# Output products as swapped 64-row halves in the common loop, an exchanged query order in pair 14, and the last norm in pieces

## The chip, the cores and the metric

The kernel runs on one core of a Trainium2 chip. Its engines are TensorE (PE in the profile, its weight loads PEld), VectorE (DVE), ScalarE (ACT), GpSimd (POOL) and SyncE (SP), which only issues DMAs here. Each takes its instructions in program order, and they wait for one another by semaphores. The metric is the device time of one execution in microseconds.

## The reference, cut to what matters

```python
x = A_x                              # 1 x 2048 x 576, 32 heads of 18
xn = layernorm(x)
q, k, v = split(xn @ wqkv)
p = softmax(q @ k.T * 18 ** -0.5)    # per head, 2048 x 2048
s = concat_heads(p @ v) @ wo
h = gelu(xn @ w_gate) * (xn @ w_up)  # 4608 wide
g = silu(h @ w_down)
return x + s * g
```

## The kernel before, in words

All products of 576-wide operands are made from 16-bit high and low parts, three matmuls in place of one. The 2048 rows are 16 row tiles of 128 (`st`), four row blocks of 512 (`sb`). The 32 heads are worked in 16 pairs (`p`), one head on partitions 0 to 63, the other on 64 to 127.

For a pair there are 64 steps (`i`): query half `qh` of 1024 rows, key tile `kt` of 128, and `half`, one of two blocks of 512 queries. In each step `qk2` (lines 1298 to 1312) makes the scores of both heads, two matmuls of 56 rows at 1302 that run at the same time, and ScalarE takes the exponential at 1308. In the common loop for the first 15 pairs (line 1580) a step also holds `qk1` (the next pair's scores again, for the row maxima, 1245 to 1253), some slots of the gate and up projection (`g_run`, `Pair`, line 472), and now and then a stage of a down projection (`DownPair`, line 762). `make_plan` (1536) lays out from a cost table how many slots and down stages each of the next steps gets, so that the gate stream ends `LEAD` steps after step 960, the end of the fifteenth pair. When a gate pair closes, the key tiles held in `pend` go through `burst` (1333): the products of P and V, four column groups of 32, in 32-bit, added on VectorE into `osum`.

A `Pair` or `DownPair` computes two results from 64-row halves. In its first stage the lower half of the array works on result a and the upper half on b, at the same time; in the second stage they change over. Between the stages stands `touch` (436), a copy of one element from PSUM on VectorE, on which the second stage waits.

At the end of a query half `norm` (1356) divides by the softmax sum (row 18 of each group). For pairs up to 13, and for the first half of the others, a chain of deferred small DMAs spreads the reciprocals (a1, a2, b, b1, b2), then c, d and e make high and low parts, and f stores them to the DRAM buffer OHL. For the second half of pairs 14 and 15 it is done in place (`direct`): a shuffle and a reciprocal of 128 x 512 on VectorE, then c, d, e at once. For pair 15 the parts stay in SBUF (`last_o`).

The last pair has a loop of its own (1658), behind `stage.open("c")`: every third step P times V by `pv` (1316), left-over down products by `down` (710, 128-row matmuls at 724), the gate's tanh and product (`queue_gate`, 800) one at a time, and, when all down products are done, the output products of `unit_out` (892) as a filler: for row tiles 8 to 15 those of pairs 0 to 14, for 0 to 5 also those of pair 15 from `last_o` (`mm_direct`, 870, line 877). An output product is 14 matmuls of 128 rows for each half of 288 columns (`mm_xw`, 486, lines 491 to 496), into one of three banks; at 923 VectorE multiplies by the gate, at 927 it adds x. Behind the loop come row tiles 6 and 7, and `final_out` (955) adds pair 15's share to row tiles 8 to 15.

Of the kernel before, what the change touches and what calls it, by code (L numbers as in the profile page):

```python
# [20 lines left out]
P = 128  # L21
# [14 lines left out]
T_XW = 0.123  # L36
TAIL_QC = 3
TAIL_K = 3
T_LAST = (NT * 28 + NT // 2 * 6 - (4 - TAIL_QC) * 2 * 34) * 0.123

# [58 lines left out]
def kernel(ctx: ExitStack, tc: tile.TileContext, x, wqkv, wo, w_gate, w_up, w_down, out):  # L99
# [610 lines left out]
    def down(tag):  # L710

        if not dnq:
            return False
        w, c, sb, si, hf = dnq.popleft()
        hs = hstate[c, sb]
        st = 4 * sb + si
        sl = slice(P * si, P * si + P)
        ms = slice(288 * hf, 288 * hf + 288)
        mt = MTile(tag, [P, 512], F32, 1)
        yy = Y[0][:, st, ms]  # L720
        k = 0
        for ft in range(2):
            for a, b in ((hs.hi, w.dhi), (hs.hi, w.dlo), (hs.lo, w.dhi)):
                nc.tensor.matmul(
                    mt.t[:, 0:288], a[:, ft, sl], b[:, ft, ms], start=(k == 0), stop=(k == 5)
                )
                k += 1
        if c == 0:
            nc.vector.tensor_scalar(yy, mt.t[:, 0:288], w.c, None, op0=ALU.mult)
        else:  # L730
            nc.vector.scalar_tensor_tensor(yy, mt.t[:, 0:288], w.c, yy, op0=ALU.mult, op1=ALU.add)
        mt.done()
        hs.left -= 1
        if hf == 1:
            dndone[c] += 1
            if c == NCH - 1 and si == 3:
                queue_gate(sb)
        return True

# [60 lines left out]
    def queue_gate(sb):  # L800

        for st in range(4 * sb, 4 * sb + 4):
            def e1(st=st):
                t = sgt[st] = stage.s.tile([P, D], F32, tag="sg", name=f"sg{st}", bufs=2)
                nc.scalar.activation(t, Y[0][:, st], AF.Tanh, scale=0.5)

            def r1(st=st):
                yy = Y[0][:, st]
                nc.vector.scalar_tensor_tensor(yy, sgt[st], 1.0, yy, op0=ALU.add, op1=ALU.mult)
                gdone[st] = 1  # L810

            gq.append(e1)
            gq.append(r1)

    sgt = {}
    gq = deque()
# [48 lines left out]
    ohl_here = []  # L865
    outk = [0]
    last_o = {}
    obt = {}

    def mm_direct(o, qh, qb, si, hf, start, stop, end=None):  # L870

        r = slice(64 * qb, 64 * qb + 64)
        sl = slice(P * si, P * si + P)
        ms = slice(288 * hf, 288 * hf + 288)
        oh, ol = last_o[qh]
        for k, (a, b) in enumerate(((oh, wod.hi), (oh, wod.lo), (ol, wod.hi))):
            nc.tensor.matmul(o, a[r, sl], b[r, ms], start=start and k == 0, stop=stop and k == 2)
            if k == 2 and end is not None:
                end()
            yield T_XW  # L880

# [3 lines left out]
    def load_ohl(qc):  # L885
        if qc in ohls:
            return
# [4 lines left out]
    def unit_out(qc, whole):  # L892

        qh = qc // 4
        until(lambda: obdone[qh] == NPAIR - 1 and W_O[0] is not None)
        if whole:
            until(lambda: qh in last_o)
        w = W_O[0]
        load_ohl(qc)
        k = OUT_ORDER.index(qc) + 1  # L900
        if k < len(OUT_ORDER):
            load_ohl(OUT_ORDER[k])
        ohl = ohls[qc]
        oh, ot, ol = ohl[:, 0:4], ohl[:, 4], ohl[:, 5:9]
        yield 0.0
        for si in range(2):
            st = 2 * qc + si
            sl = slice(P * si, P * si + P)
            xo = stage.s.tile([P, D], F32, tag="xo", name=f"xo{st}", bufs=2)
            nc.sync.dma_start(xo, x[P * st:P * st + P, :])  # L910
            if whole:
                ob = stage.s.tile([P, D], F32, tag="sg", name=f"ob{st}", bufs=2)
            else:
                ob = OB(st)
            for hf in range(2):
                ms = slice(288 * hf, 288 * hf + 288)
                mt = MTile(("ma", "mb", "mc")[outk[0] % 3], [P, 512], F32, 1)
                outk[0] += 1

                def fin(mt=mt, st=st, ms=ms, hf=hf, xo=xo, ob=ob):  # L920
                    while not gdone[st]:
                        gq.popleft()()
                    nc.vector.scalar_tensor_tensor(
                        ob[:, ms], mt.t[:, 0:288], EO, Y[0][:, st, ms], op0=ALU.mult, op1=ALU.mult
                    )
                    mt.done()
                    nc.vector.tensor_tensor(ob[:, ms], ob[:, ms], xo[:, ms], op=ALU.add)
                    if hf == 1 and whole:
                        nc.gpsimd.dma_start(out[P * st:P * st + P, :], ob)

                yield from mm_xw(
                    mt.t[:, 0:288], lambda t: oh[:, t, sl], lambda t: ol[:, t, sl], ot[:, sl], w, hf,
                    stop=not whole, end=None if whole else fin,
                )
                if whole:
                    yield from mm_direct(
                        mt.t[:, 0:288], qh, (qc % 4) // 2, st % 4, hf, False, True, fin
                    )
# [16 lines left out]
    def final_out(st):  # L955
        o = ps.tile([P, 2, 512], F32, tag=("s1", "s2")[st % 2], name=f"fo{st}")
        for hf in range(2):
            for _ in mm_direct(o[:, hf, 0:288], 1, (st - 8) // 4, st % 4, hf, True, True):
                pass
        t = ap.tile([P, D], F32, tag="P", name=f"ft{st}", bufs=6)  # L960
        nc.vector.scalar_tensor_tensor(
            t.rearrange("p (a b) -> p a b", a=2), o[:, :, 0:288], EO,
            Y[0][:, st].rearrange("p (a b) -> p a b", a=2), op0=ALU.mult, op1=ALU.mult,
        )
        eng = (nc.gpsimd, nc.vector)[st % 2]
        eng.tensor_tensor(t, t, OB(st), op=ALU.add)
        (nc.sync, nc.scalar)[st % 2].dma_start(out[P * st:P * st + P, :], t)
# [322 lines left out]
    def ptile(p, name):  # L1290
# [3 lines left out]
        if p < NPAIR - 1 and n < 64 * (NPAIR - 1) - 8 and n % 8 >= 6:  # L1294
# [19 lines left out]
    ob = [None]  # L1314

    def pv(p, qh, kt, pa, pb):
        if kt == 0:
            ob[0] = stage.p.tile([P, 512], F32, tag="pv", name=f"pv_{p}_{qh}")
        o = ob[0]
        for b, pt in enumerate((pa, pb)):  # L1320
            for h in range(2):
                qd = 64 * b + 32 * h
                c0 = 38 * kt + 19 * h
                nc.tensor.matmul(  # L1324
                    o[qd:qd + 32, :], VT[p][:, c0:c0 + 32], pt[:, h],
                    start=(kt == 0), stop=(kt == NT - 1), skip_group_check=True,
                )
        if kt == NT - 1:
            norm(p, qh, o)

    osum = {}

    def burst(todo, tag):
# [19 lines left out]
        if k1 == NT - 1:  # L1353
            norm(p, qh, None)
# [385 lines left out]
```

## Time and profile before

| | us |
|---|---|
| median of three runs (2620.77 to 2622.93) | 2620.93 |
| the profiled execution | 2621.11 |
| its span, first to last instruction | 2619.3 |
| first scores of the last pair | 2442.36 |
| last output product of the stream | 2601.86 |
| last addition (line 966) ends | 2615.83 |

The granted TensorE clock of the core is 0.992 over the span. In the profile's lists a row of the time-ordered view has start, duration, engine, line, operation and, in brackets, the idle time of the engine ahead of it with what ended it; matmul durations overlap, so what one costs is read from the distance to the next start.

### The profile page before, as it was taken

How to read it: one execution, taken by the hardware profiler on the slowest of the kernel's cores; microseconds unless marked ns; L12 is line 12 of the kernel's file. 1: busy time of each engine (PE TensorE's matmuls, PEld its weight loads, DVE VectorE, ACT ScalarE, POOL GpSimd, SP SyncE). 2: the span in 40 equal slices, each digit the busy share in tenths (PEclk: the TensorE clock that was granted, in tenths of full speed). 3: DMA queues.
4: the chain of work that ended last, by engine and by line, in shares of the span. 5: the costliest groups of instructions: out<-in, count | busy, mean ns of one | idle time of the engine just before them, and what ended most of it. 6: DMA issues, size and time to landing. Idle time of an engine off the chain costs nothing.

```text
span 2619.3 us, 59543 instructions
## 1 busy us (share of the span) xinstructions
PE 2526.9 (96%) x25220; PEld 1315.2 (50%) x25220; DVE 1930.7 (74%) x2714; ACT 1662.9 (63%) x2083; POOL 1487.4 (57%) x1418
## 2 busy tenths in 40 slices
PE   6889999999999999999999999999999999999898
PEld 5554545445545454454544554454454555555344
DVE  7587768777877778777887777777777777777444
ACT  5225666666677666767767676677666676766563
POOL 4246553576437553757667575756666575747301
PEclk9999999999999999999999999999999999999998
DMA  4430022202130022112021110102012011100123
GB/s 144 133 109 10 16 28 78 64 18 56 29 80 20 9 54 64 29 39 56 9 56 29 33 33 15 56 10 56 11 35 47 17 28 39 49 9 11 35 78 118
DMA packets 133640, 118.61 MB, mean 45 GB/s; under 512 B 60160, under 2 KB 112792, under 8 KB 133372
## 3 DMA queue, kind: packets, MB, share of 16 engines
q1 hardware_dynamic: 127740, 103.02, 15.2%
q0 software_dynamic: 3072, 8.90, 1.0%
q8 instruction: 197, 3.23, 0.5%
q10 hardware_dynamic: 2560, 2.89, 0.3%
q14 instruction: 71, 0.58, 0.1%
HBM read 84.89 MB, written 29.61 MB: 44 GB/s over the span
## 4 chain that ended last, share of the span: by engine, by line
PE 77%; DVE 10%; ACT 4%; DMA 3%; POOL 3%; issue 3%; SPq 0%; ACTq 0%; DVEq 0%; POOLq 0%
PE mb_t L472 15%; PE ma_t L472 14%; PE md_t L762 14%; PE s L1302 8%; PE md_t L1343 7%; PE s L1250 7%; PE ma_t L1343 5%; DVE PM L1253 3%; ACT P L1308 1%; DMA obr<-rd 1%; PE pv L1324 1%; DMA QT<-QD 1%; PE mc_t L491 1%; DVE m_c L252 1%; DVE osb L1351 1%
## 5 line engine op out<-in xcount | busy, mean ns | idle before, releaser
L1253 DVE TENSOR_REDUCE PM<-s 128x2 f32<-128x1024 f32 x1024 | 1250.8, 1224 | 340.4 <-PE s L1250 332.2
L1308 ACT ACTIVATE P<-s,etab 128x1024 f32<-128x1024 f32 x896 | 996.8, 1112 | 621.4 <-PE s L1302 606.1
L472 PE MATMUL ma_t<-XHT,whi_c 64*128 64x512 f16 x1440 | 542.4, 377 | 12.5 <-ACT gs L637 7.8
L472 PE MATMUL mb_t<-XHT,whi_c 64*128 64x512 f16 x1440 | 542.2, 377 | 5.2 <-ACT gv L648 2.7
L472 PE MATMUL ma_t<-XHT,wlo_c 64*128 64x512 f16 x1296 | 487.4, 376 | 0.0
L472 PE MATMUL ma_t<-XL,whi_c 64*128 64x512 f16 x1152 | 433.4, 376 | 0.0
L472 PE MATMUL mb_t<-XHT,wlo_c 64*128 64x512 f16 x1152 | 433.3, 376 | 0.0
L472 PE MATMUL mb_t<-XL,whi_c 64*128 64x512 f16 x1152 | 433.2, 376 | 0.0
L1250 PE MATMUL s<-KT,QT 54*128 54x512 f16 x2048 | 398.0, 378 | 18.5 <-DVE PM L1253 8.3
L1302 PE MATMUL s<-QT,KT 56*128 56x512 f16 x2048 | 401.0, 380 | 7.1 <-ACT P L1308 3.0
L472 PEld LDWEIGHTS <-whi_c 64*128 64x128 f16 x5184 | 276.9, 94 | 244.0 <-issue 31.8
L762 PE MATMUL md_t<-dhi_c,hhi 64*128 64x288 f16 x2216 | 327.5, 283 | 8.1 <-DVE osb L1351 5.3
L673 POOL TENSOR_SCALAR tw<-tw 128x512 f32<-128x512 f32 x144 | 90.8, 630 | 421.4 <-ACT tw L666 421.2
L762 PE MATMUL md_t<-dhi_c,hlo 64*128 64x288 f16 x2216 | 327.2, 283 | 0.0
L762 PE MATMUL md_t<-dlo_c,hhi 64*128 64x288 f16 x2216 | 326.7, 282 | 0.0
L762 PEld LDWEIGHTS <-hhi 64*128 64x128 f16 x4432 | 236.9, 94 | 137.0 <-issue 21.1
L695 POOL TENSOR_TENSOR hlo<-gv,hhi 128x512 f16<-128x512 f32 x144 | 168.6, 1171 | 225.2 <-ACT hhi L688 211.4
L1343 PE MATMUL md_t<-P,VT 128*32 128x512 f32 x2368 | 274.4, 596 | 0.4 <-DVE y L782 0.3
L1302 PEld LDWEIGHTS <-KT 56*128 56x128 f16 x2048 | 124.8, 94 | 263.0 <-issue 175.4
L660 POOL TENSOR_TENSOR tw<-gs 128x512 f32<-128x512 f32 x144 | 152.0, 1056 | 120.9 <-ACT gs L637 120.5
L782 DVE SCALAR_TENSOR_TENSOR y<-md_t,c_c,y 128x576 f32<-128x576 f32 x261 | 210.5, 806 | 1.2 <-PE md_t L762 1.2
L472 PEld LDWEIGHTS <-wlo_c 64*128 64x128 f16 x2592 | 139.6, 94 | 120.2 <-issue 1.0
(271 smaller groups left out, 4048.4 us busy)
## 6 DMA issues: line engine op xcount, KB each, us to landing
draw_c<-in_B_w_down SPq DMA_DIRECT2D x18, 576.0 KB
raw_c<-in_B_w_gate SPq DMA_DIRECT2D x18, 512.0 KB
raw_c<-in_B_w_up SPq DMA_DIRECT2D x18, 512.0 KB
obr<-rd SPq DMA_DIRECT2D x30, 256.0 KB
KT<-KD SPq DMA_DIRECT2D x32, 224.0 KB
QT<-QD SPq DMA_DIRECT2D x32, 216.0 KB
VS<-vst POOLq DMA_DIRECT2D x16, 304.0 KB, 3.8
VT<-VS SPq DMA_DIRECT2D x16, 304.0 KB
```

What stands on the lines that cost most here:

```text
L252: nc.vector.tensor_reduce(w.m5[:, t:t + 1], w.raw[:, t], op=ALU.max, axis=AX.XY, apply_absolute_value=True)
L472: nc.tensor.matmul(o, lw, xx, start=self.stage == 0 and self.k == 0, stop=self.stage == 1 and self.k == self.slots - 1, skip_group_check=True,
L660: gp.tensor_tensor(st["t"], st["g"], st["g"], op=ALU.mult)
L673: gp.tensor_scalar(st["t"], st["t"], 1.0, 1.0, op0=ALU.mult, op1=ALU.add)
L695: gp.tensor_tensor(hs.lo[:, ft], st["v"], hs.hi[:, ft], op=ALU.subtract)
L762: nc.tensor.matmul(self.t.t[:, hf, 0:288], a[r, ft, sl], b[r, ft, 288 * hf:288 * hf + 288], start=self.stage == 0 and k == 0, stop=self.st ...
L782: nc.vector.scalar_tensor_tensor(yy, y, w.c, yy, op0=ALU.mult, op1=ALU.add)
L1250: nc.tensor.matmul(s1[:, h], QT[p][r, P * qt:P * qt + P], KT[p][r, 512 * kb:512 * kb + 512], start=True, stop=True)
L1253: nc.vector.tensor_reduce(PM[p][:, :, qt, kb:kb + 1], s1, op=ALU.max, axis=AX.X)
L1302: nc.tensor.matmul(s2[:, h], KT[p][r, P * kt:P * kt + P], QT[p][r, 512 * qb:512 * qb + 512], start=True, stop=True)
L1308: nc.scalar.activation(pt, s2, AF.Exp, scale=ETAB[j0])
L1343: nc.tensor.matmul(t.t[qd:qd + 32, :], VT[p][:, c0:c0 + 32], pt[:, h], start=kt == k0, stop=kt == k1, skip_group_check=True,)
```

## The change

The loop of the last pair goes: the common loop runs over all 16 pairs. When the gate stream has ended, a step takes a branch of its own, with at most one down stage and some output slots.

- `LEAD` is 0 in place of 10, and the planner's choice of steps for a gate pair has slightly other bounds.
- In pair 14 the query halves are worked in exchanged order (`qh = 1 - qh`). Its norms both go through the deferred chain.
- The output products are `OutPair` objects: 64-row halves, two stages of 14 slots (17 with pair 15's terms, which stand on one half alone), a `touch` between them. Units take turns in PSUM: one wide tile `md`, or `ma` and `mb`. The product with the gate stays on VectorE, the addition of x goes to POOL (a whole row tile), the stores of row tiles 0 to 7 to SP's queue.
- A gate's tanh and product are issued in the same step, on odd steps.
- The norm of pair 15 is nine pieces (shuffle, four reciprocals of 128 columns, c, d, e, g), popped one in a step, two per stage behind the loop.
- `final_out` pairs row tiles 8 + k and 12 + k, whose terms stand on different halves, and six of its eight additions run on POOL.
- Buffers: sigmoid tiles and outputs in the QT buffers, x in the KT buffers, P tiles of the last pair also in PX.

```diff
+            self.q = []
+            for half in range(2):
+                hf = half ^ self.stage
+                r = slice(64 * half, 64 * half + 64)
+                terms = []
+                for t in range(4):
+                    for xx, ww in ((oh, w.hi), (oh, w.lo), (ol, w.hi)):
+                        terms.append((xx[r, t, sl], ww[r, t, hf, :]))
+                terms += [(ot[r, sl], w.hi[r, 4, hf, :]), (ot[r, sl], w.lo[r, 4, hf, :])]
+                if self.whole and half == st % 8 // 4:
+                    terms += direct_terms(st, hf)
+                self.q.append((self.o[hf], terms))
...
+            if self.stage == 0:
+                if self.wide:
+                    touch(self.t[0].t[0:1, :, 0:1])
+                else:
+                    for o in self.o[1:] if last else self.o[::-1]:
+                        touch(o[0:1, 0:1])
+            self.stage += 1
+            if self.stage == 2:
+                self.evac()
...
+        def evac(self):
+            st = self.st
+            while not gdone[st]:
+                for fn in gq.popleft():
+                    fn()
...
+            nc.gpsimd.tensor_tensor(ob, ob, self.xo, op=ALU.add)
+            if self.whole:
+                nc.sync.dma_start(out[P * st:P * st + P, :], ob)
```

The readiness of a unit, the pacing, and the branch of a step behind the gate stream (`more` is true up to pair 14):

```diff
+    def out_ready(st):
+
+        if st // 4 not in gated or obdone[st // 8] < NPAIR - 1 or W_O[0] is None:
+            return False
+        return st >= 8 or 0 in last_o
...
+            elif u.stage == 1 and u.k == u.slots:
+                if blocks[0] <= tail.end:
+                    return
+                u.begin()
...
-    for p in range(NPAIR - 1):
+    for p in range(NPAIR):
...
+            if p == NPAIR - 2:
+                qh = 1 - qh
...
+            if gs.left == 0 and gs.pair is None and not gs.closed and not plan:
+                load_ohl(OUT_ORDER[0])
+                u = tail.unit
+                late = False
+                d = dn is not None or (
+                    len(dnq) > 1 and not (more and 57 < i < 61) and held < 5 and (u is None or not u.wide)
+                )
...
+                run = pend and dn is None and (held >= 6 or kt == NT - 1 and half == 1 and i < 63)
+                run = run or held >= 8
...
+                if run:
+                    wide = u.wide if u is not None else not tail.wide
+                    flush(("ma", "mb") if dn is not None or wide else ("md", "md"))
+                else:
+                    if gq and i % 2:
+                        for fn in gq.popleft():
+                            fn()
+                    if final_norm:
+                        final_norm.popleft()()
+                    if d or more:
+                        out_run(5 if d else 10)
+                    else:
+                        credit = min(credit + 9, 18)
...
+    while units or tail.unit is not None:
+        blocks[0] += 1
+        for _ in range(2):
+            if final_norm:
+                final_norm.popleft()()
+        out_run(99, True)
+        subtick()
```

The norm and the planner:

```diff
-        direct = qh == 1 and p >= NPAIR - 2
...
-        if direct:
-            for fn in (c, d, e, g if last else f):
-                fn()
+        if last:
+            final_norm.extend([shuffle, *(lambda k=k: inverse(k) for k in range(4)), c, d, e, g])
...
-    LEAD = 10
+    LEAD = 0
...
-        for n in range(max(4, math.floor(size) - 1), min(9 - held, 7, math.ceil(size) + 1) + 1):
+        for n in range(max(4, min(6, math.floor(size) - 1)), min(9 - held, 7, max(4, math.ceil(size) + 1)) + 1):
```

More of the change, by code (lines that the diff above doesn't have):

```diff
@@ L35 @@
 FREE = {"A": 4.0, "V": 4.0, "T": 1.3}
[L36 to L39, printed above, removed]
 class Deferred:
@@ L708 @@
     dndone = [0] * NCH
[L710 to L738, printed above, removed]
     class DownPair:
@@ L931, in unit_out @@
[L931 to L938, printed above, removed]
+            for t in self.t:
+                t.done()
+            nc.gpsimd.tensor_tensor(ob, ob, self.xo, op=ALU.add)
@@ L1312, in qk2 @@
         return pt
[L1314 to L1329, printed above, removed]
+    final_norm = deque()
     osum = {}
@@ L1599 @@
                 qk1(kp, next(items))
-            if i == 62:
+            if i == 62 and more:
                 steps[2]()
@@ L1696 @@
[L1696 to L1711 removed]
+    while gq:
+        for fn in gq.popleft():
+            fn()
```

372 lines of the change are left out of this document (187 added, 185 removed).

## The prediction

> **What bounds the kernel now.** I read the page first: its busy shares and the chain that ended last.
>
> ```profile
> span 2619.3 us, 59543 instructions
> PE 2526.9 (96%) x25220; PEld 1315.2 (50%) x25220; DVE 1930.7 (74%) x2714; ACT 1662.9 (63%) x2083; POOL 1487.4 (57%) x1418
> PE 77%; DVE 10%; ACT 4%; DMA 3%; POOL 3%; issue 3%; SPq 0%; ACTq 0%; DVEq 0%; POOLq 0%
> ```
>
> TensorE is busy 96% of the span and carries 77% of the chain, so only two things pay: TensorE time that can go, and stretches in which it waits. The change leaves the first fifteen pairs of heads nearly as they are, so I read the busy time by stretch behind 2442 us, where the last pair's scores begin (columns: stretch, its length, busy time and instructions of PE, PEld, DVE, ACT, POOL, granted TensorE clock, DMA share, GB/s).
>
> ```profile
> 2442.00:2494.00 52.00, 41.93 (x299) 19.22 (x294) 22.71 (x36) 26.04 (x33) 16.07 (x15) 0.93 0.17 44
> 2494.00:2592.00 98.00, 98.00 (x722) 46.12 (x724) 34.42 (x68) 59.49 (x59) 2.78 (x5) 1.00 0.29 94
> 2592.00:2602.60 10.60, 10.08 (x81) 6.24 (x74) 9.00 (x13) 1.23 (x2) 1.08 (x2) 1.00 0.17 57
> 2602.60:2619.30 16.70, 9.47 (x47) 5.23 (x43) 12.00 (x14) 0.00 (x0) 6.14 (x5) 0.60 0.46 177
> ```
>
> Three places: a stretch with 10 us of idle TensorE (2442 to 2494), a full one, and an end of 16.7 us at a clock of 0.60. In the full stretch ScalarE has 59.5 us of work in 98, so it could run much shorter before exponentials bind. The profiled execution took 2621.11 us, 1.8 over its span and 0.2 over the median of 2620.93; I work in the span and add 1.8.
>
> **The change part by part. 1: the stall at the last boundary goes.** The time-ordered list there:
>
> ```profile
> 2443.99 3.35 DVE L1371 RECIPROCAL obr<-obr 128x512 f32<-128x512 f32 x1
> 2444.75 0.38 PE L1302 MATMUL s<-QT,KT 56*128 56x512 f16 x2
> 2448.10 0.63 ACT L1397 ACTIVATE onh<-osb 128x512 f16<-128x512 f32 x1 [8.08 <-DVE osb L1393]
> 2450.88 0.58 PE L472 MATMUL ma_t<-XHT,whi_c 64*128 64x512 f16 x1 [5.74 <-ACT gs L637]
> 2453.03 0.58 PE L472 MATMUL mb_t<-XHT,whi_c 64*128 64x512 f16 x1 [1.57 <-ACT gv L648]
> 2455.95 0.38 PE L472 MATMUL mb_t<-XL,whi_c 64*128 64x512 f16 x1
> 2456.16 0.38 PE L472 MATMUL mb_t<-XHT,wlo_c 64*128 64x512 f16 x1
> ```
>
> The norm of pair 14's second half is done in place: VectorE's reciprocal takes 3.35 us, ScalarE's FIFO stands 8.08 us behind its result, and the exponentials and the gate and up copies queue behind that, so TensorE idles 5.74 + 1.57 = 7.3 us. Then it runs slowly: from 2453.03 to 2455.95 seven slots of two matmuls take 2.92 us, 0.42 each, against 0.21 for the next (2455.95 to 2456.16); 1.5 us more. After the change this norm goes through the chain of small DMAs that all earlier pairs use, and ScalarE never waits for it in its FIFO. With the query order exchanged the half that ends last is the first one (rows 0 to 7), whose products are due only behind 224 slots of others. -8.8 us.
>
> **2: no change of array shape around the output products.** In the last pair a 56-row score pair, then a 128-row product, then a score pair; in the common loop a score pair and a 64-row product:
>
> ```profile
> 2495.07 0.29 PE L491 MATMUL ma_t<-whi_wo,ohl 128*128 128x288 f16 x1
> 2495.28 0.39 PE L1302 MATMUL s<-QT,KT 56*128 56x512 f16 x2
> 2495.61 0.30 PE L491 MATMUL ma_t<-whi_wo,ohl 128*128 128x288 f16 x1
> 2284.64 0.39 PE L1250 MATMUL s<-KT,QT 54*128 54x512 f16 x2 [0.17 <-DVE PM L1253]
> 2284.85 0.30 PE L762 MATMUL md_t<-dhi_c,hhi 64*128 64x288 f16 x2
> 2285.47 0.30 PE L762 MATMUL md_t<-dhi_c,hlo 64*128 64x288 f16 x2
> 2285.59 0.38 PE L472 MATMUL ma_t<-XHT,whi_c 64*128 64x512 f16 x1
> 2596.71 0.29 PE L496 MATMUL mc_t<-wlo_wo,ohl 128*128 128x288 f16 x1
> 2596.92 0.11 PEld L877 LDWEIGHTS <-onh 64*128 64x128 f16 x2 [0.24 <-issue]
> ```
>
> Into the 128-row form the score takes 0.33 us of issue, into the 64-row form 0.21; out of it 0.21 against 0.12; and the direct terms (L877) pay the same 0.21. So each crossing costs 0.10 us. In the list from 2457 to 2602.6 I count 62 crossings one way and 54 back: -11.6 us. The products keep their price: 28 issues of 0.12 for a row tile before; after it 2 stages of 14 slots, each slot two half matmuls, and such a slot takes 0.12 in the rows above (2284.85 to 2285.47 is five). The down products at L724 get the form of L762 too; their crossings are in the count.
>
> **3: fewer bursts of P times V.** The loop before has 22 groups of one or two key tiles; the common loop collects three (held of 6), some 11 groups, each with two crossings of the array into and out of 32 columns at 0.10: -2.2 us. The matmuls keep their price.
>
> **4: the end.** Before, the last eight row tiles take 16.7 us. After it the two halves' products run together (24 slots in place of 48 matmuls), six of eight additions go to POOL, two to VectorE. Rows of the stretch behind 2442 us:
>
> ```profile
> L961 DVE SCALAR_TENSOR_TENSOR ft<-fo,EO,y 128x576 f32<-128x576 f32 x8 | 6.5, 812 | 1.1 <-PE fo L877 1.1
> L966 POOL TENSOR_TENSOR ft<-ft,ob 128x576 f32<-128x576 f32 x4 | 5.6, 1396 | 5.8 <-DVE ft L961 5.8
> L923 DVE SCALAR_TENSOR_TENSOR ob<-ma_t,EO,y 128x288 f32<-128x288 f32 x11 | 5.7, 517 | 18.3 <-PE ma_t L877 10.5 <-PE ma_t L496 7.8
> 2614.83 1.00 DVE L966 TENSOR_TENSOR ft<-ft,ob 128x576 f32<-128x576 f32 x1
> ```
>
> First six slots 0.7 + 0.2, first product 0.8, six POOL additions of 1.40 = 8.4, 0.6 for what is left of the last unit's product (two of 0.52) ahead of them; then 3.5 from the last addition to the end as before (2615.8 to 2619.3): 14.2, so -2.5 us (0 to -3).
>
> **5: what TensorE waits for while down products finish**, 2460 to 2494:
>
> ```profile
> 2460.00:2494.00 34.00, 31.24 (x224) 15.18 (x220) 15.38 (x28) 20.04 (x25) 10.82 (x10) 1.00 0.06 19
> ```
>
> 2.8 us idle. They run beside output slots now, which fill such gaps: -1 (0 to -2.8).
>
> **6: the swap.** Between the stages of an output unit the halves change banks, and a one-element copy on VectorE must lie between. The loop before has such copies in its gate and down pairs:
>
> ```profile
> L440 DVE COPY touch<-md_t x277: 135/138/148, 225.3 to 2438.0; 1x2 f32<-1x2 f32 x139
>   PE mb_t L472: 3.8, 6
>   PE md_t L762: 1.8, 6
> L809 DVE SCALAR_TENSOR_TENSOR y<-sg,y 128x576 f32<-128x576 f32 x16 | 12.9, 806 | 4.0 <-ACT sg L805 3.8 <-issue 0.3
> L805 ACT ACTIVATE sg<-y 128x576 f32<-128x576 f32 x16 | 10.8, 675 | 0.0
> L1308 ACT ACTIVATE P<-s,etab 128x1024 f32<-128x1024 f32 x64 | 71.2, 1112 | 52.1 <-PE s L1302 52.1
> ```
>
> Twelve such waits, 5.6 us, 0.47 each, among hundreds of copies; the others were covered by scores between the stages. By these rows 16 swaps cost 0 to 7.5 us. New is a gate's tanh and product popped in one step: VectorE's product (0.81) waits for a tanh (0.68) behind an exponential (1.11), and a copy issued behind it waits up to 2.6 us. A handful of swaps meet one. Together 0 to 10; I take +5, nearer the covered rows.
> The rule against this form is in the Trainium skill, TensorEngine Tiling (Array Packing), Gotcha 1: row tiles may not use one PSUM bank at the same time, and the program must order them. The trace agrees in that a copy at line 440 stands between the stages of each pair. So the copy cannot be left out; were every one of the 16 swaps uncovered, the sum would be 2.5 us higher by the 0.47 above.
>
> **7: a hole in the middle of the pair.** Rows 8 to 15 give 8 x 28 = 224 slots; at 5 a step beside a down stage and 9 otherwise, none in a burst step, they last to about step 35 to 40. Rows 0 to 7 open when nine pieces of the first half's norm have been popped, one a step behind the burst at step 31: about step 41. In 0 to 6 steps TensorE has only a score pair (0.2) under an exponential (1.11): 0 to +5, I take +2.5. Some 95 slots (11.6 us) are left behind the loop, against a last norm of about 7 us.
>
> **8: the first load.** The output tiles' operands (576 KB) are fetched when the gate stream has ended, which may be a step before use; the old loop had 40 us.
>
> ```profile
> 2453.32 2.35 SPq L890 DMA_DIRECT2D ohl<-OHL  x2
> 2456.00:2460.00 4.00, 4.00 (x35) 1.56 (x33) 1.19 (x3) 1.11 (x1) 0.00 (x0) 1.00 1.05 284
> ```
>
> Issue 1.2 us, 2 us for 576 KB at 284 GB/s, and some start: 0 to +5, I take +2.
>
> **9: work moved.** With LEAD 0 the planner ends the gate stream inside pair 14, not ten steps later.
>
> ```profile
> 2442.30:2470.00 27.70, 10.47 (x74) 4.13 (x74) 0.88 0.31 81
> ```
>
> These 74 matmuls (line 472 alone), 37 slots of 0.21 = 8 us, go into a loop that TensorE bounds too: 0 (0 to +3). Additions to POOL and loads into the QT and KT buffers lie beside. Were the cover gone, a POOL addition is late by 1.4 us, and behind it on SP's queue the next row tile's x, which is due a unit (3.4 us) later.
>
> **The sum:** -8.8 - 11.6 - 2.2 - 2.5 - 1 + 5 + 2.5 + 2 = -16.6: a span of 2602.7, a time of **2604.5**. Every cost at nothing and every gain full: -28, 2593. Every cost full and gains at their least: 1 to 3 alone, -22.6 + 23, 2621.
>
> **The rivals.** *The costs are all covered:* 2594. For it: 98 of 98 us busy in the old loop, twelve uncovered swaps in all of before. Against: hole and load have no cover that I see.
> *The halves save nothing*, the 0.10 being paid elsewhere (loading two half weights for each slot): -16.6 + 11.6, 2616. Against it the same pair of forms at 2284.64 in the common loop.
> *Slower, by the swap as a wall:* VectorE's queue is never short when a stage ends, because products, burst additions, norm pieces and gates that wait for ScalarE stand ahead of the copy. At its price of 2.5 us for each of 16 swaps it is 40 in place of 5: 2639; slower than before by what can be told once a swap costs more than 1.7 us. For it: the 2.6 us chain above. Against: VectorE busy 34 of 98 us, and gates are only in the first half.
> *The last norm stands bare:* if the slots run out in the loop, shuffle, reciprocals, product, copy and difference leave TensorE idle:
>
> ```profile
> 2593.57 0.72 DVE L1370 STREAM_SHUFFLE obr<-osb 128x512 f32<-128x512 f32 x1
> 2594.32 3.35 DVE L1371 RECIPROCAL obr<-obr 128x512 f32<-128x512 f32 x1
> 2599.10 0.69 DVE L1401 TENSOR_TENSOR onl<-osb,onh 128x512 f16<-128x512 f32 x1 [0.70 <-ACT onh L1397]
> ```
>
> From 2593.57 to 2599.79 that is 6.2 us, and the 24 final slots at half clock 2.9: 2613.6. Against: the 95 slots.
>
> **How the numbers follow.** Forecast 0.54 (2598 to 2612), covered costs 0.16, no saving by halves 0.13, wall 0.12, bare norm 0.05. A measurement tells 0.2%, 5.2 us, from no change: faster below 2615.7, slower above 2626.2. Faster: 0.54 + 0.16 + 0.05 and 0.05 of the third, whose 2616 lies at the edge: 0.80; same 0.08; slower 0.12. Range 2593 to 2620.
>
> **What would show it.** Right: at the last boundary no ScalarE wait for an output norm, TensorE's clock at 1.00 there; score pairs 0.21 from the next output matmul; about 11 bursts in the last pair; under 15 us from the first direct product to the end. Wrong: waits of TensorE for the copies over 10 us in all, idle TensorE at the start of the last pair (load) or near its middle (hole) over 5 us, or gate matmuls still behind the boundary. A main loop longer by more than 12 us (the 8 of part 9 and its bound) would overturn the sum.

## The result and the profile after

| | us | ratio to before, 95% interval |
|---|---|---|
| before, median of 20 runs | 2620.53 | |
| after, median of 20 runs (2613.98 to 2618.92) | 2615.72 | 0.9982 [0.9975, 0.9989] |
| the profiled execution of after; its span | 2615.07; 2613.3 | |

The kernel is faster, by 4.8 us and not by the 16 forecast. The interval excludes a ratio of 1, but the prediction had put the least change that it could tell at 5.2 us (2615.7), and the result stands on that line. The page of the changed kernel, its span and busy shares:

```profile
span 2613.3 us, 60781 instructions
PE 2509.3 (96%) x25800; PEld 1326.2 (51%) x25800; DVE 1933.6 (74%) x2719; ACT 1661.2 (64%) x2081; POOL 1509.2 (58%) x1428
```

TensorE works 17.6 us less (2526.9 to 2509.3), but the span lost only 6.0. The busy time by stretch tells where the rest is. The common loop of the first fifteen pairs (first scores to the first scores of the last pair) and all behind it, before:

```profile
212.60:2442.40 2229.80, 2196.06 (x22471) 1115.70 (x22472) 1700.97 (x2332) 1503.39 (x1851) 1372.71 (x1265) 1.00 0.14 35
2442.40:2619.30 176.90, 159.07 (x1138) 76.78 (x1134) 78.13 (x129) 86.75 (x94) 26.07 (x27) 0.94 0.26 85
```

The same after, with the last pair cut at its last scores and at the last output and final products:

```profile
214.00:2462.30 2248.30, 2209.94 (x22641) 1124.91 (x22641) 1716.28 (x2348) 1507.55 (x1858) 1384.57 (x1276) 1.00 0.14 35
2462.30:2580.50 118.20, 107.87 (x1308) 64.94 (x1306) 47.32 (x88) 79.03 (x83) 21.27 (x17) 0.99 0.28 83
2580.50:2600.20 19.70, 17.91 (x245) 12.59 (x240) 13.19 (x24) 1.88 (x3) 5.78 (x5) 1.00 0.29 91
2600.20:2613.30 13.10, 0.25 (x5) 0.00 (x0) 5.34 (x7) 0.00 (x0) 8.99 (x6) 0.67 0.52 203
```

Three terms make the 6.0. The start, which the change leaves alone, is 1.4 later (212.6 to 214.0). The loop is 18.5 longer: TensorE is busy 13.9 more (2209.94 - 2196.06) and idle 4.6 more (38.4 against 33.7). What is behind the loop, called the tail below, is 25.9 shorter (176.9 to 151.0). The 13.9 is work that LEAD 0 moved from the tail into the loop, so it cancels: the tail's own gain is 12.0, and 4.6 of it is given back as idle time in the loop.

The boundary in the changed kernel, busy time of 15 us around it, and then the time-ordered list of an output stage (TensorE alone, one half of each pair):

```profile
2455.00:2470.00 15.00, 14.34 (x178) 8.90 (x177) 4.59 (x10) 11.12 (x14) 7.14 (x9) 1.00 0.29 83
```

```profile
2527.78 0.28 PE L900 MATMUL mb_t<-whi_wo,ohl 64*128 64x288 f16 x1
2527.88 0.40 PE L1326 MATMUL s<-QT,KT 56*128 56x512 f16 x2
2528.10 0.28 PE L900 MATMUL ma_t<-wlo_wo,ohl 64*128 64x288 f16 x1
```

TensorE is busy 14.3 of 15 us at clock 1.00 where it stood 7.3 us and ran at half speed. The score pair follows a half product by 0.10 and the next one comes 0.22 later: the crossings of the array's shape are gone, as forecast.

What TensorE waits for in the last pair (total, times, longest):

```profile
PE mb_t L900 <- DVE touch L436: 6.2, 5, 3.5
PE md_t L728 <- DVE osb L1359: 1.5, 3, 0.5
PE s L1326 <- ACT P L1332: 1.1, 3, 0.7
PE md_t L900 <- DVE touch L436: 0.9, 2, 0.8
```

The copies between the stages hold TensorE for 7.1 us, half of it in one place. The list there:

```profile
2528.96 0.40 PE L1326 MATMUL s<-QT,KT 56*128 56x512 f16 x2
2529.08 0.72 DVE L926 SCALAR_TENSOR_TENSOR ob<-md_t,EO,y 128x576 f32<-128x576 f32 x1
2529.39 0.67 ACT L771 ACTIVATE sg<-y 128x576 f32<-128x576 f32 x1
2529.88 1.40 POOL L938 TENSOR_TENSOR ob<-ob,xo 128x576 f32<-128x576 f32 x1 [7.24 <-DVE ob L926]
2530.09 1.79 DVE L775 SCALAR_TENSOR_TENSOR y<-sg,y 128x576 f32<-128x576 f32 x1 [0.30 <-ACT sg L771]
2531.81 0.94 DVE L1378 RECIPROCAL obr<-obr 128x128 f32<-128x128 f32 x1
2532.67 0.08 DVE L436 COPY touch<-mb_t 1x1 f32<-1x1 f32 x1
2532.83 0.28 PE L900 MATMUL mb_t<-whi_wo,ohl 64*128 64x288 f16 x1 [3.47 <-DVE touch L436]
2533.32 0.45 PE L900 MATMUL mb_t<-whi_wo,ohl 64*128 64x288 f16 x1
2533.56 0.44 PE L900 MATMUL mb_t<-wlo_wo,ohl 64*128 64x288 f16 x1
```

The stage's last product was issued at 2528.86; its copy runs at 2532.67. Ahead of it in VectorE's FIFO stand an output product (L926, 0.72), the gate's product (L775, 1.79) and a piece of the last norm (0.94). The gate's product waits for ScalarE's tanh (L771) only 0.30 us; the larger part is its own length, which is not the usual one:

```profile
L775 DVE SCALAR_TENSOR_TENSOR y<-sg,y x16: 757/759/1794, 2466.6 to 2554.7; 128x576 f32<-128x576 f32 x16
```

Its shortest, median and longest durations are 757, 759 and 1794 ns. Twelve of the sixteen take 0.76 us. The other four began while an operation of GpSimd was running and took 0.81, 0.90, 1.10 and 1.79; each ended about 0.6 us behind the end of GpSimd's. Here it is the addition of x (L938), which the change moved to GpSimd: it runs from 2529.88 to 2531.28, and the product, begun at 2530.09, ends at 2531.88. So some 1.0 us of the 3.5 is GpSimd's. No run keeps these additions on VectorE, so what they cost in all is open.

The last two rows of the list show a second price: matmuls 0.24 apart, not 0.12. The stretches of that place (the granted clock is the third number from the end):

```profile
2526.00:2529.00 3.00, 3.00 (x51) 2.58 (x47) 2.27 (x3) 2.32 (x4) 0.00 (x0) 1.00 0.03 8
2529.00:2532.80 3.80, 0.36 (x5) 0.06 (x1) 3.50 (x6) 2.07 (x3) 1.40 (x1) 1.00 0.00 0
2532.80:2534.30 1.50, 1.47 (x15) 1.16 (x15) 0.82 (x1) 0.00 (x0) 0.00 (x0) 0.58 0.00 0
2534.30:2536.00 1.70, 1.70 (x12) 0.40 (x12) 0.00 (x0) 0.95 (x1) 0.00 (x0) 0.50 0.00 0
2536.00:2538.00 2.00, 2.00 (x20) 0.36 (x12) 0.00 (x0) 0.16 (x1) 0.00 (x0) 0.88 0.00 0
```

After 3.5 us without work the clock is halved for some 3.4 us. The time lost is 1.5 x 0.42 + 1.7 x 0.50 + 2.0 x 0.12 = 1.7 us. So the copies cost 7.1 + 1.7 = 8.8.
The Trainium skill, TensorE: Matmul & The Clock Gate (Part 1: The HAM clock gate), says that an idle window of about 3.4 us brings half the clock and a busy one of that length ends it; these stretches agree.
A shorter wait was enough too. In the common loop of the same execution TensorE waits 2.35 us for an addition of VectorE (ended at 747.63), and the clock is halved behind it:

```profile
745.28:747.63 2.35, 0.01 (x2) 0.00 (x0) 2.35 (x5) 1.10 (x2) 0.00 (x0) 1.00 0.26 85
747.88:751.29 3.41, 3.41 (x20) 1.49 (x18) 1.43 (x2) 0.16 (x1) 0.00 (x0) 0.50 0.30 83
```

This wait stands in all ten profiles with LEAD 0 and is followed by half clock in each; one of 2.05 us near 2211 is followed by it in five of the ten, and not in this one.

The end, in the time-ordered list:

```profile
2593.59 1.40 POOL L938 TENSOR_TENSOR ob<-ob,xo 128x576 f32<-128x576 f32 x1 [4.84 <-DVE touch L436]
2595.02 0.34 SPq L940 DMA_DIRECT2D out<-ob  x1
2595.45 0.39 SPq L870 DMA_DIRECT2D xo<-in_A_x  x1
2595.53 0.28 PE L900 MATMUL ma_t<-wodh,onl 64*128 64x288 f16 x1
2598.62 1.40 POOL L938 TENSOR_TENSOR ob<-ob,xo 128x576 f32<-128x576 f32 x1 [3.63 <-DMA xo<-in_A_x]
2599.98 9.21 POOL L990 TENSOR_TENSOR ft<-ft,ob 128x576 f32<-128x576 f32 x6
```

The load of the last row tile's x (L870) stands on SP's queue behind a store (L940) that waits for GpSimd's addition, so it is issued at 2595.45 and GpSimd idles 3.63 us for it; only then come its six additions, 9.2 us in a row. From the last product of the last unit, one of pair 15's terms, to the end it is 17.7 us (2595.53 to 2613.3); before it was 16.9 (line 877, from 2602.35 to 2619.3).

### The profile page after: what moved, and what is told of

The parts are those of the page before. It is cut to its first block, busy times and chain, and to the rows that moved or that the text cites. A ratio compares the mean times of both kernels' runs of the same rounds, so it can differ in the third digit from the quotient of the medians.

```text
span 2613.3 us, 60781 instructions
## 1 busy us (share of the span) xinstructions
PE 2509.3 (96%) x25800; PEld 1326.2 (51%) x25800; DVE 1933.6 (74%) x2719; ACT 1661.2 (64%) x2081; POOL 1509.2 (58%) x1428
## 4 chain that ended last, share of the span: by engine, by line
PE 79%; DVE 10%; ACT 4%; issue 2%; DMA 2%; POOL 2%; SPq 0%; ACTq 0%; POOLq 0%; DVEq 0%
PE mb_t L468 16%; PE ma_t L468 15%; PE md_t L728 15%; PE md_t L1351 9%; PE s L1326 8%; PE s L1274 8%; PE ma_t L1351 6%; DVE PM L1277 3%; ACT P L1332 1%; DVE osb L1359 1%; DVE m_c L248 1%; PE md_t L900 1%; PE mb_t L900 1%; PE mb_t L1351 1%; DMA QT<-QD 1%
## 5 line engine op out<-in xcount | busy, mean ns | idle before, releaser
L728 PE MATMUL md_t<-dhi_c,hhi 64*128 64x288 f16 x2304 | 341.6, 283 | 7.1 <-DVE osb L1359 2.2
L728 PE MATMUL md_t<-dhi_c,hlo 64*128 64x288 f16 x2304 | 341.3, 282 | 0.0
L728 PE MATMUL md_t<-dlo_c,hhi 64*128 64x288 f16 x2304 | 340.8, 282 | 0.0
L728 PEld LDWEIGHTS <-hhi 64*128 64x128 f16 x4608 | 247.3, 94 | 141.0 <-issue 22.6
L1351 PE MATMUL md_t<-P,VT 128*32 128x512 f32 x2472 | 290.2, 598 | 0.3 <-ACT P L1334 0.2
L748 DVE SCALAR_TENSOR_TENSOR y<-md_t,c_c,y 128x576 f32<-128x576 f32 x272 | 219.2, 806 | 8.3 <-PE md_t L728 8.2
```

What stands on the lines that cost most here:

```text
L728: nc.tensor.matmul(self.t.t[:, hf, 0:288], a[r, ft, sl], b[r, ft, 288 * hf:288 * hf + 288], start=self.stage == 0 and k == 0, stop=self.st ...
L748: nc.vector.scalar_tensor_tensor(yy, y, w.c, yy, op0=ALU.mult, op1=ALU.add)
L1351: nc.tensor.matmul(t.t[qd:qd + 32, :], VT[p][:, c0:c0 + 32], pt[:, h], start=kt == k0, stop=kt == k1, skip_group_check=True,)
```

## The experiments

"Tail" is the stretch from the last pair's first scores to the end, "loop" the common loop, each from one profiled execution. Such an execution lies up to 2.5 us from the median of its run (run 2: 2608.89 against 2606.39), so tails that differ by less than about 2 us tell little. Kernels sent together share the runs of the kernel before.

| run | median us | ratio to before, 95% interval | loop | tail |
|---|---|---|---|---|
| 1 full rows | 2611.45 | 0.9965 [0.9953, 0.9978] | 2245.4 | 150.5 |
| 2 gate apart | 2606.39 | 0.9946 [0.9934, 0.9959] | 2248.7 | 144.5 |
| 3 end | 2613.94 | 0.9971 [0.9960, 0.9983] | 2245.9 | 150.9 |
| 4 LEAD 10, old bounds | 2613.49 | 0.9972 [0.9961, 0.9983] | 2225.9 | 171.5 |
| 5 = 1 + 2 | 2613.77 | 0.9974 [0.9964, 0.9984] | 2248.2 | 149.6 |
| 6 before, norm deferred | 2616.41 | 0.9983 [0.9974, 0.9992] | 2229.8 | 170.6 |
| 7 old query order | 2633.85 | 1.0053 [1.0041, 1.0066] | 2249.1 | 169.5 |
| 8 = 2 + 3 | 2605.87 | 0.9948 [0.9935, 0.9960] | 2248.1 | 143.2 |
| 9 = 8, LEAD 10, old bounds | 2604.99 | 0.9939 [0.9927, 0.9951] | 2225.8 | 164.2 |
| 10 norm at once | 2622.35 | 1.0003 [0.9994, 1.0012] | 2248.0 | 158.8 |
| 11 before, LEAD 5 | 2619.85 | 0.9996 [0.9987, 1.0005] | 2232.6 | 170.6 |
| 12 = 8, additions 5 and 3 | 2606.63 | 0.9945 [0.9933, 0.9958] | 2248.6 | 144.5 |
| 13 = 8, old bounds | 2607.81 | 0.9951 [0.9937, 0.9966] | 2248.9 | 143.2 |
| 14 = 8, LEAD 5, old bounds | 2600.58 | 0.9923 [0.9906, 0.9939] | 2231.5 | 155.4 |
| 15 = 8, LEAD 10 | 2598.06 | 0.9914 [0.9899, 0.9929] | 2224.6 | 157.8 |

**Halves, gates and the copies: runs 1, 2, 5.** Run 1 makes the output products of 128 rows, a column half in each stage, without the copy:

```diff
-            for half in range(2):
-                hf = half ^ self.stage
-                r = slice(64 * half, 64 * half + 64)
...
+            hf = self.stage
...
+                    terms.append((xx[:, t, sl], ww[:, t, hf, :]))
...
-                        touch(o[0:1, 0:1])
```

> The changed kernel with its output products as 128-row matmuls again, one half of the columns per stage, same slots, no copy between the stages. Theory (a crossing of array shapes costs 0.10 us): some 110 crossings come back, +11 us, and the 7.1 us that TensorE waits for copies in the output units go: +4 us on 2615.7, so 2620, ratio to the kernel before 0.9998. Rival (the halves save nothing): only the waits go, 2608.6, ratio 0.9955.

Run 2 keeps the halves and issues a gate's tanh and its product one step apart:

```diff
-            gq.append((e1, r1))
+            gq.append((e1,))
+            gq.append((r1,))
...
-                    if gq and i % 2:
+                    if gq:
```

> The changed kernel with a gate's tanh and its product issued one step apart. Theory (copies between stages stand on VectorE behind a product that waits for a tanh behind an exponential): the 7.1 us of waits for copies fall to 2 or 3, 2611, ratio 0.9965. Rival (VectorE's queue is as long without it, or other waits take the time): 2615 to 2616, ratio 0.9982.

Run 5 has both edits.

> 128-row output products (as in e1) and gates in two steps (as in e2) together. Theory (the gates cost only through the copies between stages, which 128-row products don't have): the same as e1 within 2 us, 2611, ratio 0.9965; so slower than e2 by 4 to 5 us, which is the price of some 90 crossings less the waits that e2 has left. Rival (gates also hold TensorE by VectorE's other work): both gains add, 2602, ratio 0.993.

Run 1 was expected at 2620 if a crossing costs 0.10 us, or at 2608.6 if it costs nothing, and came out at 2611.45: beside the changed kernel's paired gates the halves earn nothing. Halves and full rows tie in the tail (151.0 and 150.5), and in the medians full rows are 4.3 us ahead, of which 2.9 lie in the loop, which the edit doesn't touch. With the gates apart the halves are 5.1 shorter (144.5 against 149.6), 7.4 in the medians. Taking the gate steps apart is worth 6.5 in the tail and 9.3 in the medians where there are copies; where there are none the tail is 0.9 shorter and the median 2.3 longer. So the paired gates cost through the copies. By how much through the wait for the tanh, and by how much through what VectorE and GpSimd happen to do at that moment, the runs don't separate: in run 2 the gate product nearest to that place begins at 2528.45, 0.16 ahead of GpSimd's addition, waits for nothing and takes 0.75; another (2512.95) still meets an addition, takes 1.83, and a copy behind it is waited for 0.92. Run 2's waits in the last pair:

```profile
PE mb_t L901 <- DVE touch L436: 2.4, 4, 0.9
PE md_t L901 <- DVE touch L436: 0.9, 2, 0.8
```

3.3 us in place of 7.1, none above 0.92, and the clock stays at 1.00 where it fell before:

```profile
2529.00:2532.80 3.80, 2.89 (x35) 1.34 (x35) 1.93 (x4) 3.06 (x4) 1.45 (x1) 1.00 0.00 0
2532.80:2534.30 1.50, 1.50 (x18) 0.28 (x10) 0.13 (x1) 0.00 (x0) 0.00 (x0) 1.00 0.00 0
```

The 3.8 us of waits and the 1.7 of half clock make 5.5 of the 6.5. And the halves' gain of 5.1 stands beside 3.3 us of copies that the full rows don't have, so the crossings that they save are worth about 8.4 in the output products (10.7 by the medians).

**The norm in pieces: run 10.** All nine pieces are issued in one step. They belong to the last pair's norm, not to pair 14's, as the expectation has it:

```diff
-            final_norm.extend([shuffle, *(lambda k=k: inverse(k) for k in range(4)), c, d, e, g])
+            def once():
+                for fn in pieces:
+                    fn()
+
+            final_norm.append(once)
```

> The changed kernel with all nine pieces of pair 14's last norm issued in one step of the last pair, not one piece a step. Theory A (a copy that releases TensorE to the next 64-row stage waits behind whatever VectorE has been given; four reciprocals, a shuffle and the two products are some 8 us of VectorE in one place): the longest wait of TensorE behind a copy grows from 3.5 to 6 us or more, and the time is 3 to 6 us above the changed kernel's 2615.7, so 2618 to 2622. Theory B (the norm is off the path, the waits are those of the gate tanh and product alone): within 1.5 us of the changed kernel, 2614 to 2617.

The run is 6.6 us above the changed kernel and no faster than before: without the spreading the gain of 4.8 is gone. The waits of the last pair and the stretches around the longest:

```profile
PE md_t L900 <- DVE touch L436: 11.1, 3, 5.7
PE mb_t L900 <- DVE touch L436: 3.8, 4, 1.6
```

```profile
2524.00:2530.20 6.20, 0.59 (x9) 0.25 (x5) 5.44 (x8) 2.06 (x3) 0.00 (x0) 0.88 0.15 56
2530.20:2532.00 1.80, 1.67 (x16) 1.18 (x17) 0.84 (x3) 0.87 (x2) 0.00 (x0) 0.50 0.00 0
2532.00:2534.00 2.00, 2.00 (x18) 1.32 (x16) 0.00 (x0) 1.11 (x1) 0.00 (x0) 0.50 0.00 0
2534.00:2536.00 2.00, 2.00 (x22) 1.38 (x19) 0.82 (x1) 0.00 (x0) 0.77 (x1) 0.60 0.03 8
```

It is the same mechanism at a larger size: VectorE works 5.4 of 6.2 us ahead of a copy, TensorE 0.6, and then TensorE works some 5.4 us at half clock.

**The boundary and the query order: runs 6 and 7.** Run 6 is the kernel before with pair 14's second norm through the deferred chain; run 7 is the changed kernel without the exchange:

```diff
-        direct = qh == 1 and p >= NPAIR - 2
+        direct = qh == 1 and p >= NPAIR - 1
```

```diff
-            if p == NPAIR - 2:
-                qh = 1 - qh
```

> The kernel before with the norm of pair 14's second half through the deferred DMA chain, nothing else. Theory (step 1: ScalarE's FIFO no longer stands behind the in-place norm; 7.3 us of idle and 1.5 of slow clock go): 2612, ratio 0.9966. Rival (the output products then wait for the later store, or another wait at the boundary takes its place): 2618 to 2621, ratio 0.999 to 1.

> The changed kernel with pair 14's queries in the usual order. Theory (row tiles 8 to 15 open only some 17 steps into the last pair, and beside a down stage of 0.74 us and scores of 0.21 an exponential of 1.11 then bounds): 5 to 8 us slower than the changed kernel, 2622, ratio 1.0005. Rival (the left-over down products fill those steps anyway): 2616, ratio 0.9982.

Run 6 shortens the tail by 6.3 and the median by some 4, between its two expectations. ScalarE's wait for the norm is gone, but the gate stream still crosses the boundary there, and TensorE still waits for ScalarE's gate and up copies:

```profile
PE mb_t L472 <- ACT gv L648: 1.8, 1, 1.8
PE mb_t L724 <- ACT gv L648: 1.3, 1, 1.3
```

Run 7 is 18 us slower than the changed kernel, and slower than before; both its expectations missed. Its longest waits:

```profile
PE ma_t L900 <- DMA ohl<-OHL: 7.7, 1, 7.7
PE mb_t L900 <- DVE touch L436: 5.5, 5, 2.4
PE md_t L900 <- DVE touch L436: 5.3, 4, 1.8
```

In the old order rows 8 to 15, the first to be worked, are those whose norm has just been sent through the small DMAs; TensorE waits 7.7 us for them, the copies cost 10.8 us in place of 7.1, and the granted clock is 0.92 over the first 64 us of the last pair. So the changed kernel needs the exchange with the deferred chain. The kernel before doesn't: in run 6, where the first output product comes some 45 us behind the boundary (2489.6), the chain pays in the old order.

**The end: runs 3, 8, 12.** Run 3 puts the stores of rows 0 to 7 on POOL's queue and shares the last additions four and four; run 8 is this and the gates apart; run 12 has five and three:

```diff
-                nc.sync.dma_start(out[P * st:P * st + P, :], ob)
+                nc.gpsimd.dma_start(out[P * st:P * st + P, :], ob)
...
-            eng = nc.vector if k == 3 else nc.gpsimd
+            eng = nc.vector if half else nc.gpsimd
```

> The changed kernel with the stores of row tiles 0 to 7 on POOL's queue in place of SP's, and four of the eight last additions on VectorE in place of two. Theory (the last load of x stands behind a store on SP's queue and holds POOL 2.4 us, and then six additions of 1.40 us in a row end it): the end is 3 to 4 us shorter, 2612, ratio 0.9968. Rival (the end is bound by the last stores, or VectorE and POOL hold each other up): less than 1 us, ratio 0.998.

> Gates in two steps (e2) and the end of e3 together in the changed kernel. Theory (they lie in different places, so the gains add): 9.3 and 1.8 us off 2615.7, 2604.6, ratio 0.9939. Rival (the last stores take what the end gains): 2606.4, ratio 0.9946.

> The changed kernel as in the eighth run, but of the last eight additions five go to GpSimd and three to VectorE (the changed kernel: six and two; the eighth run: four and four). In the eighth run VectorE ended last, in the kernel as changed GpSimd. If the two engines end together at five and three, the end is 0.5 to 1 us shorter than the eighth run's 16.3: 2605 to 2605.6. If GpSimd's chain of five at 1.5 us each ends last again, 0.5 to 1 us longer: 2606.4 to 2607.

The wait for x is gone in run 3 and the end is 16.3 us against 17.7, but the tail is 150.9 against 151.0 (the last pair's steps took 1.3 us more there; behind the same wait of 3.47 us for a copy the clock was halved for 5.4 us of work in place of 3.4), and its median is 1.8 below the changed kernel's. Run 8 is 1.3 shorter in the tail than run 2 and 0.5 in the median, within the two intervals. Run 12 gains nothing over run 8: its end is 17.7 us again. The time is that of its second expectation, but the reason isn't: GpSimd's five additions end at 2599.91, and VectorE ends last, at 2603.70. So the store's place on SP's queue and the split of the additions, which were not tried apart, are worth 1.8 us at most together, and no split came near the end of 14.2 us that was forecast. The traces show why: the two engines don't add side by side. In run 3 the four additions on VectorE take 0.76, 1.99, 1.40 and 1.21 us, and the three long ones began while GpSimd was adding. In run 12 VectorE's first one began at 2595.16 among GpSimd's five, took 5.37 us in place of 0.76, and ended 0.62 behind the last of them.

**LEAD and the planner's bounds: runs 4, 9, 11, 13, 14, 15.** The edits are `LEAD` and the range of steps for a gate pair ("old bounds" is the line of before).

> The changed kernel with LEAD 10 and the old bounds of the planner. Theory (the denser plan costs TensorE 4 to 6 us of waits in the common loop beside the 14 us of work that it moves): the last pair begins 18 to 20 us earlier and takes 14 us longer, 2611, ratio 0.9965. Rival (the plan costs nothing, and output units that may only start when the gate stream has ended lose time in the last pair): 2616 to 2620, ratio 0.9985 to 1.

> The changed kernel with the gate pieces apart and the shorter end, as in the eighth run, and besides LEAD 10 with the planner bounds of the kernel before. It tells whether the denser common loop of LEAD 0 pays. Theory A (the denser loop costs more than the work moved: the main loop measured 2247.7 us on the mean of seven profiles with LEAD 0 and 2228.5 on three with LEAD 10, 19.2 apart, for 13.9 us of TensorE work moved): the main loop falls by 19, the last pair takes back the 13.9 and no waits that it did not have, so about 2605.9 - 5 = 2601, range 2599 to 2604. Theory B (the last pair is bound by ScalarE and the copies where it is long, and the work comes back with waits of its own, as in the fourth run, where the tail grew by 20.5 for the 22.3 won): 2605.9 - 2 = 2604 to 2608.

> The kernel before with LEAD 5 in place of 10, nothing else. It measures the price of a denser common loop without the rest of the change. Theory A (each step of LEAD less costs waits in the loop, 5.3 us over ten steps): the main loop is longer by about half of 19.2, so 9 to 10 us, the last pair is shorter by only the 7 us of work, and the time is 2 to 3 us above the kernel before: 2622 to 2625, ratio 1.0008 to 1.0015. Theory B (work moved costs the same in both places): 2620 to 2621.5. Theory C (the last pair has waits that leave with the gate stream): 2 to 5 us below the kernel before, 2615 to 2618.

> The changed kernel with the gate pieces apart and the shorter end (as in the eighth run, 2605.9 us, common loop 2248.1), LEAD 0, but with the planner bounds of the kernel before. Theory A (the new bounds cost the loop its extra waits): the common loop is about 2225.8 + 13.9 + 1.7 (16 products of P and V that the ninth run left behind) = 2241, at most 2243, and the time falls by 5 to 7 us to 2599 to 2601. Theory B (LEAD 0 itself costs them, because the denser loop has no slack for VectorE): the common loop stays at 2246 to 2250 and the time within 2 us of 2605.9.

> As the run before it, with LEAD 5. By theory A the common loop takes 2225.8 + 7.0 + at most 1.7 = 2233 to 2235 and the time is near that of the two ends, 2599 to 2604. By theory B the loop takes about 2232.6, as in the eleventh run, where half of the work moved cost only 2.8 us, and the time is the least of all, 2597 to 2602, because the cost of density comes only with the last five steps. Both near the ninth run's 2605.0 would mean that the plan of the loop decides little.

> The ninth run's kernel (LEAD 10, old bounds: common loop 2225.8 us, 2605.0 in all) with the planner bounds of the changed kernel. Theory A: the loop is longer by 5 to 8 us, 2231 to 2234, and the time 2610 to 2613. Theory B: the loop stays at 2224 to 2229 and the time within 2 us of 2605.0.

The loop alone, run 13 (LEAD 0, old bounds), run 14 (LEAD 5) and run 15 (LEAD 10, new bounds), each its own row:

```profile
213.10:2462.00 2248.90, 2209.77 (x22641) 1125.96 (x22640) 1716.20 (x2348) 1507.51 (x1858) 1384.42 (x1276) 1.00 0.14 35
```

```profile
211.80:2443.30 2231.50, 2201.22 (x22548) 1126.49 (x22548) 1706.96 (x2344) 1504.88 (x1854) 1377.99 (x1270) 1.00 0.14 35
```

```profile
215.30:2439.90 2224.60, 2193.09 (x22463) 1116.04 (x22464) 1700.47 (x2332) 1503.47 (x1851) 1372.87 (x1264) 1.00 0.14 35
```

Idle TensorE in the loop is 39.1, 30.3 and 31.5 us; it is 37.7 in run 8, 31.9 in run 9, 33.7 before and 38.4 after. LEAD 0 in place of 10 costs 7.3 us of waits with the old bounds (run 13 against run 9) and 6.2 with the new (run 8 against run 15); LEAD 5 costs none (run 14). So it is LEAD, not the bounds, and only its last five steps, as the theories B of runs 13 and 14 had it. Run 15's loop came out by its theory B too; its time fits neither theory. Run 11 says the same of the kernel before: LEAD 5 moves 7 us of work for a loop 2.8 longer, and the time stays as it was. The bounds matter elsewhere: run 15 beats run 9 by 6.9 us with a loop only 1.2 shorter. Both leave 16 products of P and V for behind the loop, so these are not the difference. But in run 9 a copy waited behind the last norm for 3.63 us, where the longest such wait of run 15 is 1.10:

```profile
2562.00:2565.70 3.70, 0.14 (x2) 0.00 (x0) 2.97 (x7) 0.63 (x1) 0.00 (x0) 0.98 0.00 0
2565.70:2569.00 3.30, 3.23 (x28) 2.75 (x28) 0.08 (x2) 0.00 (x0) 1.94 (x2) 0.51 0.11 43
```

Once more it is 3.6 us of waiting and 3.3 at half clock. Why the bounds move this wait was not followed further. Run 4, the changed kernel with LEAD 10 and the old bounds, came out between its two expectations: it took back as tail (20.5) nearly all that its loop gained (22.4), and the copies' waits were still in it.

Run 15 is the fastest, 2598.06 us, though its interval overlaps that of run 14: the changed kernel with LEAD 10, the gate's two steps apart, the stores on POOL's queue and four additions on each engine. It is 17.7 us under the changed kernel and 22.3 under the one before.

## Why the prediction was right in direction and wrong in size

The span was to fall by 16.6 and fell by 6.0. The forecast of 2604.5 failed; the range (2593 to 2620) held. Three terms of the sum were too favourable: the work moved (step 9), the swap (step 6) and the end (step 4). In the last two stands a cost that the prediction put at nothing: GpSimd's additions and VectorE's hold each other up.

- **Step 6, the swap, was mis-sized.** It gave +5, "nearer the covered rows". The copies cost 8.8, 7.1 in waits and 1.7 in halved clock. The prediction had named the paired gate as a wait of up to 2.6 us that "a handful of swaps meet", and a wall as the way to a slower kernel; it took the price of a swap from a loop where scores stand between the stages. (Its rows there also leave out three waits of 1.7 us, for other tiles.) Seven swaps waited, five of them under 1 us, but one stood behind an output product, a gate and a piece of the norm for 3.5 us, longer than the dearest case the prediction had. It left out that such a wait is paid again in clock, and that GpSimd's additions, which step 9 let "lie beside", hold VectorE: 1.0 of the 3.5 us.
- **Step 9, work moved, was mis-sized.** It gave 0, bound 3. The loop's idle time rose by 4.6, the largest miss; runs 8, 9, 13 and 15 show that LEAD 0 does it. It also counted 74 gate matmuls (8 us) alone; 48 down slots moved too, so 13.9, which cancels. The sign that it had named, a loop longer by more than 12 us, came at 18.5. Why the last five steps cost more than the first is argued, not shown: the plan must fit more work per step, and VectorE's row maxima and additions come due closer together.
- **Step 4, the end, was mis-sized.** It gave -2.5 and measured +0.8 (17.7 against 16.9). It started GpSimd's six additions behind the last product; they start behind an addition of x that waits 3.63 us for its load, and two of them take 1.92 in place of 1.40, beside an addition of VectorE. Step 9 had named this queue, at a price of 1.4 us for one late addition and not at the end.
- **Step 8, the load, was not due.** It gave +2; the first load of the operands was issued at 2449.7, 12.6 us ahead of the last pair's first scores, and nothing waited for it: 0.
- **Steps 1, 2, 3, 5 and 7** were put at -21.1 together. The tail's own -12.0 less the 0.8 of step 4 and the 8.8 of step 6 leaves -21.6. That is what is left over, not a measurement, and its closeness is in part luck, since one profiled execution lies up to 2.5 us from the median. Singly: step 1 was right as a mechanism, though run 6 shows that the norm alone gives 6.3 and leaves waits for the gate stream's copies, and run 7 that the changed kernel needs the exchange of the query halves, which the prediction did not price by itself. Step 2's price of a crossing stands in the rows, and runs 2 and 5 give 8.4 for the output products; the 11.6 counted the down products too. Step 7's hole is small: waits for exponentials are 1.1 us in all. Step 3's bursts came out as 12 groups in place of 22, 11 forecast; their time was not measured alone, nor was step 5.

The misses add up: 4.6 (step 9) + 3.3 (step 4) + 3.8 (step 6) - 2 (step 8) - 0.5 (the others, by what is left over) + 1.4 (the start, which lies between 211.8 and 215.3 in the rows above, of kernels that share it) = 10.6, which is 16.6 - 6.0.

Of the rivals, "the halves save nothing" named about the right time (2616) by luck, for the wrong reason: runs 2 and 5 show that the halves do save once the gates are apart.

## What to carry to other kernels

Where a product of halves needs a small copy on another engine before its second stage, the copy is only as quick as that engine's FIFO: look at what will be issued ahead of it, spread it, and look at what GpSimd does at that moment. Price a TensorE wait of over 3 us here as the wait and 1.6 to 2.7 us of lost clock (the changed kernel, runs 3, 9 and 10). Whether work moved out of a tail into a full loop is free depends on how much is moved: the first 7 us cost the loop no idle time (run 14 against run 9), the next 7 cost 7 to 9 (runs 8 and 13 against run 14). Try the step between (LEAD 5) before the whole.

## What the runs showed of the hardware

The clock is lost in the middle of a full-speed stream by one wait: 3.47 us idle in the changed kernel and in run 3, 3.63 in run 9 and 5.7 in run 10 were each followed by a granted clock near 0.50 while TensorE worked 3.3 to 5.4 us, and run 2, with no wait above 0.92 in that stretch, kept 1.00. The length of the wait alone doesn't decide: in the loop 2.35 us was followed by it in ten profiles of ten, 2.05 us in five of ten.

An operation of VectorE with both operands in SBUF that begins while GpSimd is adding ends about 0.6 us after that addition of GpSimd: gate products of 1.79 us (the changed kernel) and 1.83 (run 2), each 0.76 by itself. An addition in run 12 ended only 0.62 us behind the last of GpSimd's row of additions and took 5.37. A product that reads PSUM (L979) kept its 0.81 us beside GpSimd's additions.
